# The first gather table: scaling in place on ScalarE and subtracting on GpSimd, in sixteen pieces

## The chip, the cores and the metric

The kernel runs on one core of one Trainium2 chip. The core has a matrix engine (TensorE, "PE" in the profile), three engines for elementwise work (VectorE "DVE", ScalarE "ACT", GpSimd "POOL"), and SyncE ("SP"), which here issues DMAs. Every engine works through its own list of instructions in order; semaphores hold an instruction back until what it needs has been done by another engine. The metric is the device time in microseconds of one execution; lower is better.

## The reference, cut to what matters

The reference propagates node features seven times over a random graph of N = 10000 nodes and E = 160000 edges (D = 128 features), and then runs one self-attention block over the eight "hop" vectors of each node.

```
K = 7
h = x; toks = [x]
for _ in range(K):
    msg = h[src] * deg_inv_sqrt[src, None] * deg_inv_sqrt[dst, None]
    h = segment_sum(msg, dst, N)
    toks.append(h)
...                       # layer norm, attention over the 8 tokens, readout
```

## The kernel before, in words

**Tables.** A hop gathers rows of a table of 79 blocks of 128 nodes. Each table row holds a node's 128 scaled features as two float16 halves, "high" (columns 0 to 127) and "low" (columns 128 to 255): high is the scaled feature rounded to float16, low is what the rounding left. The scale is a power of two, so it can be applied exactly. `tab0` is the table of the first hop. Its float32 source `y` is `x` times `deg_inv_sqrt`; it lies in the storage of `tab1` (the profile therefore calls it `tab` too), which the first hop overwrites later.

**Stages.** Four stages follow each other: pass A (about 45 to 364 us of the span) sorts the 160000 edges by block of their destination, in 25 chunks of 50 columns; `decode` and the first `place` unpack them; seven hops (from about 411 us) gather and scatter on TensorE; attention comes last.

**Pass A, one chunk.** The tile library's scheduler merges the instruction streams of neighbouring chunks; what it gave each engine is a fixed list. In terms of tiles, chunk after chunk:

- VectorE makes a one-hot `oh` (line 204, 128x3950), TensorE counts it into `U` (line 301, 50 matmuls of 79 columns), ScalarE copies that to `U2` (line 314).
- VectorE multiplies `ux = oh * U2` (line 217); TensorE sums it into `R` (lines 222 and 223); VectorE reduces `R` to ranks `rk` (line 226) and compares them into `ro0`, `ro9`, `ro17` (line 337, three instructions).
- The right-hand sides `o0`, `o9`, `o17` are filled by VectorE (line 210) and, for `o9` and `o17`, half by ScalarE with 32 small instructions (line 327).
- TensorE multiplies `ro` by `o` into `ta` (line 341, 50 matmuls, 18 with `o0`, 16 with `o9`, 16 with `o17`), and VectorE adds `ta` up into `TT` (line 305).

`o0`, `o9` and `o17` have one buffer each, so the next chunk's may be written only once TensorE has used them. `oh` has two buffers, so the `oh` of a chunk may be written only once ScalarE has read the one two chunks back.

**The first table** is made inside pass A: at `ch == 2` the program calls `first_table`. A maximum over all of `y` (line 190) gives the scale `q`; then four times, for 20, 20, 20 and 19 blocks, `to_table` (lines 160 to 163) makes the halves and `rows` (lines 165 to 170) has SyncE write them to DRAM (`tabd`, and `tabh` for the last blocks). The first to read them there are the gathers on GpSimd's queue (line 591) in hop 1. The scheduler put ScalarE's part of the table in the middle of its line 327 work for chunk 2, after 13 of the 32 instructions.

Of the kernel before, what the change touches and what calls it, by code (L numbers as in the profile page):

```python
# [14 lines left out]
AF = mybir.ActivationFunctionType  # L15
ALU = mybir.AluOpType
# [27 lines left out]
class Hops:  # L44
# [114 lines left out]

    def to_table(self, y, tab, q, t0, t1):  # L160

        self.nc.scalar.activation(tab[:, t0:t1, 0:128], y, AF.Copy, scale=q)
        self.nc.vector.scalar_tensor_tensor(tab[:, t0:t1, 128:256], y, q, tab[:, t0:t1, 0:128], op0=ALU.mult, op1=ALU.subtract)

    def rows(self, i, tab, t0, t1, eng):
        eng.dma_start(self.tabd[i][t0 * 128:t1 * 128, :].rearrange("(t p) w -> p t w", p=128), tab[:, t0:t1, :])
# [1261 lines left out]
```

## Time and profile before

| | |
|---|---|
| time, median of 3 runs | 4046.84 us (4045.33 to 4047.72) |
| the profiled execution's own time | 4047.25 us |
| its span, from the first to the last instruction | 4045.5 us |
| busy share PE / PEld / DVE / ACT / POOL | 91% / 75% / 75% / 69% / 46% |
| mean granted TensorE clock | 0.975 |

How to read it: a timeline row gives start and duration in us, engine, line, operation, `out<-in`, the shapes, and in brackets the engine's idle time just before and what ended it. Several instructions may be merged into one row (`x4`); its time then runs from the first start to the last end. Neighbouring instructions of an engine overlap a little in the records (by about 0.1 us), so the distance between two starts, not the duration, is what an instruction adds to its engine's list. A row of a window table gives, for a stretch of the span, its length, the busy time of each engine, the granted TensorE clock (1.00 is full speed), the DMA share and GB/s. The chain of waits is the sequence of work that ended last, followed back from the end.

### The profile page before, as it was taken

To read this page: it belongs to the slowest core of one execution; us is meant where nothing else is said; L and a number is where in the kernel's file an instruction comes from. 1 tells how busy PE (TensorE), PEld (TensorE's weight loads), DVE (VectorE), ACT (ScalarE), POOL (GpSimd) and SP (SyncE) were. 2 spreads that over 40 slices of the span, in tenths; PEclk is the share of its full clock that TensorE was granted. 3 is DMA by queue.
4 is the path that set the end of the run, shared out by engine and by line. 5 is a ranking of instruction groups with operands and counts; after the bars stand their busy time and mean duration, and the time that the engine had idled before them with its cause. 6 is when DMAs were issued, how large, how long until landed. Compare 5 with 4: busy or idle time off the path is not lost.

```text
span 4045.5 us, 166006 instructions
## 1 busy us (share of the span) xinstructions
PE 3685.5 (91%) x69042; PEld 3017.9 (75%) x69042; DVE 3041.9 (75%) x6973; ACT 2785.1 (69%) x6934; POOL 1853.3 (46%) x2493
## 2 busy tenths in 40 slices
PE   4776899999889999999999999999999999999996
PEld 3665677777667777777777777777777887888885
DVE  8999988888766666666666666666664555999998
ACT  6674577777656666666666666666666778888884
POOL 0000344444465556555665565665556662222222
PEclk8988999999999999999999999999999999999997
DMA  3100454555466666666666666666667661222220
GB/s 97 37 2 1 158 171 164 175 169 170 142 180 184 186 187 184 185 187 179 188 186 185 184 186 186 185 186 185 185 182 223 187 185 52 73 78 79 73 74 23
DMA packets 320887, 590.64 MB, mean 146 GB/s; under 512 B 56779, under 2 KB 214697, under 8 KB 314873
## 3 DMA queue, kind: packets, MB, share of 16 engines
q1 hardware_dynamic: 281225, 501.46, 40.0%
q0 software_dynamic: 35616, 73.01, 8.0%
q8 instruction: 542, 8.88, 0.9%
q10 hardware_dynamic: 3280, 5.45, 0.5%
q14 instruction: 224, 1.84, 0.1%
HBM read 451.66 MB, written 128.06 MB: 143 GB/s over the span
## 4 chain that ended last, share of the span: by engine, by line
PE 65%; DVE 22%; issue 4%; another core or an unknown queue 3%; DMA 3%; ACT 2%; POOL 1%; SPq 0%; DVEq 0%; POOLq 0%; ACTq 0%
PE acc L645 21%; PE p L667 20%; DVE eb L670 5%; PE acc L631 3%; PE pv L1088 3%; PE po L1099 3%; PE pu L1077 3%; PE ta L341 2%; PE tm L420 2%; DVE s L617 2%; PE pt L1067 1%; DVE ro L337 1%; DVE oh L204 1%; DVE R L210 1%
## 5 line engine op out<-in xcount | busy, mean ns | idle before, releaser
L670 ACT CAST eb<-p 128x512 f16<-128x512 f32 x3494 | 1822.3, 599 | 824.7 <-PE p L667 522.1
L667 PE MATMUL p<-tab,w 128*32 128x256 f16 x39312 | 1306.9, 275 | 108.1 <-DVE eb L670 64.2
L667 PEld LDWEIGHTS <-w 128*32 128x32 fp8e3 x39312 | 997.1, 96 | 336.8 <-issue 280.8
L645 PE MATMUL acc<-eb,w 128*128 128x256 f16 (+1 forms) x9828 | 1198.0, 273 | 0.1
L645 PEld LDWEIGHTS <-w 128*128 128x128 fp8e4 x9828 | 949.1, 98 | 153.4 <-issue 38.8
L670 DVE CAST eb<-p 128x512 f16<-128x512 f32 x1420 | 928.5, 686 | 76.3 <-PE p L667 64.0
L617 DVE TENSOR_REDUCE s<-acc 128x128 f32<-128x256 f32 x553 | 234.2, 424 | 706.3 <-PE acc L645 342.5
L591 POOL DMA_INDIRECT og<-tabh,oidx x546 | 601.5, 1102 | 351.3 <-POOL og L601 175.7
L591 POOL DMA_INDIRECT og<-tabd,oidx x546 | 562.6, 1030 | 303.5 <-issue 123.7
L703 POOL TENSOR_SCALAR r<-s,ctok 128x128 f32<-128x128 f32 x553 | 399.3, 722 | 574.1 <-DVE s L617 523.4
L327 ACT ACTIVATE o<-oh,d2s 128x79 f16<-128x79 f16 x800 | 204.7, 372 | 80.8 <-PE ta L341 80.8
L1113 ACT ACTIVATE junk<-tab 128x128 f32<-128x128 f32 x625 | 245.1, 394 | 0.0
L1099 PEld LDWEIGHTS po<-v,pT 128*128 128x128 f32 x1250 | 161.0, 195 | 42.7 <-issue 27.4
L1171 POOL TENSOR_TENSOR p<-e,in 128x512 f32<-128x512 f32 (+1 forms) x40 | 40.8, 1021 | 331.5 <-DVE e L1169 300.5
L341 PE MATMUL ta<-o,ro 128*128 128x158 f16 x1250 | 119.8, 268 | 77.8 <-DVE ro L337 77.8
L697 DVE SCALAR_TENSOR_TENSOR tab<-s,c,tab 128x128 f16<-128x128 f32 x474 | 170.3, 359 | 14.6
L1088 PE MATMUL pv<-Wv,xT 128*128 128x131 f32 x1250 | 175.5, 283 | 4.7 <-ACT xT L1068 4.1
L341 PEld LDWEIGHTS <-ro 128*128 128x128 f16 x1250 | 114.7, 114 | 82.1 <-DVE ro L337 82.0
L1099 PE MATMUL po<-v,pT 128*128 128x128 f32 x1250 | 168.7, 279 | 5.5 <-DVE o L1105 5.5
L1088 PEld LDWEIGHTS pv<-Wv,xT 128*128 128x128 f32 x1250 | 152.8, 191 | 21.4 <-issue 8.2
L125 POOL MEMSET eb<- 128x520 f16 x10 | 8.2, 852 | 341.1 <-PE ta L341 341.1
L631 PE MATMUL acc<-og,w 128*128 128x256 f16 x546 | 153.9, 282 | 0.0
(314 smaller groups left out, 4650.8 us busy)
## 6 DMA issues: line engine op xcount, KB each, us to landing
w<-gsd SPq DMA_DIRECT2D x468, 592.0 KB
gsd<-w SPq DMA_DIRECT2D x78, 592.0 KB
rb<-srow SPq DMA_DIRECT2D x78, 576.0 KB
tok<-r SPq DMA_DIRECT2D x546, 64.0 KB
tab<-tok SPq DMA_DIRECT2D x273, 128.0 KB
tabd<-tab SPq DMA_DIRECT2D x469, 64.0 KB
og<-tabh,oidx POOLq DMA_INDIRECT x546
og<-tabd,oidx POOLq DMA_INDIRECT x546
```

What stands on the lines that cost most here:

```text
L327: A.activation(o[:, j - a, NK:, i], oh[:, j, :, i], AF.Copy, scale=d2s[:, c0:c0 + 1])
L341: T.matmul(ta, ro[:, j - a, :, i], o[:, j - a, :, i], start=j + i == 0, stop=j + i == NP)
L591: self.nc.gpsimd.indirect_dma_start(out=o, out_offset=None, in_=src[0] if i == NI else src[1], in_offset=bass.IndirectOffsetOnAxis(ap=self ...
L617: self.nc.vector.tensor_reduce(s, acc[:, 0:256].rearrange("p (h d) -> p d h", h=2), axis=X, op=ALU.add)
L631: T.matmul(acc[0][:, :256], W, og()[i], start=start, stop=stop)
L645: T.matmul(acc[0][:, :m], w[:, J * 128:(J + 1) * 128], e[:, j, :m], start=first and J == 0, stop=J == NG - 1 and not (first or late))
L667: T.matmul(p[32 * q:32 * q + 32, j], w[:, NJ * 128 + s * CAP:NJ * 128 + (s + 1) * CAP].bitcast(F8G), tab[:, s, :], start=True, stop=True)
L670: (A.copy if evac(jj) else V.tensor_copy)(e[:, :n, 0:256], p[:, :n].rearrange("p j h d -> p j (h d)"))
L703: self.nc.gpsimd.tensor_scalar(r, s, ct[:, t:t + 1], None, op0=ALU.mult)
L1088: T.matmul(p[:, g - a, :], S[i]["xT"][:, g, :], Wv, start=True, stop=True)
L1099: T.matmul(p[:, g - a, :], PT[i % 2][:, g, :], S[i]["v"][:, g, :128], start=True, stop=True)
L1113: A.activation(j, S[i]["x"][:, g, :], AF.Square, bias=S[i]["x"][:, g, 0:1], scale=-1.0, accum_out=S[i]["sq"][:, g:g + 1])
```

## The change

`to_table` now goes through its blocks five at a time (16 pieces: 15 of five blocks, 640 elements in each partition, and one of four, 512). In each piece ScalarE multiplies `y` by `q` in place in float32 (after's line 165), ScalarE copies the product to the high half, rounding it to float16 (line 166), and GpSimd subtracts the high half from the product into the low half (line 167). Before, ScalarE made the high half straight from `y`, and VectorE computed `y * q - high`, in four instructions each. The DMAs, `first_table` and everything else are the same; line numbers behind `to_table` are four higher in the changed kernel.

```diff
     def to_table(self, y, tab, q, t0, t1):
 
-        self.nc.scalar.activation(tab[:, t0:t1, 0:128], y, AF.Copy, scale=q)
-        self.nc.vector.scalar_tensor_tensor(tab[:, t0:t1, 128:256], y, q, tab[:, t0:t1, 0:128], op0=ALU.mult, op1=ALU.subtract)
+        for i in range(0, t1 - t0, 5):
+            a, b = t0 + i, min(t1, t0 + i + 5)
+            z = y[:, i:i + b - a]
+            self.nc.scalar.activation(z, z, AF.Copy, scale=q)
+            self.nc.scalar.copy(tab[:, a:b, 0:128], z)
+            self.nc.gpsimd.tensor_tensor(tab[:, a:b, 128:256], z, tab[:, a:b, 0:128], op=ALU.subtract)
```

The scheduler's lists for TensorE and SyncE are the same as before. Those of the other three differ only around the table. VectorE's list before, from the last instructions ahead of the table on; the number at a name's end tells buffers apart (`oh_872`, `o9_1161`, `o17_1162`, `ta_1200` belong to chunk 2, `oh_1085`, `o0_1334`, `ux_1313`, `rk_1332` to chunk 3, `oh_1259` to chunk 4), and the brackets name the engines whose semaphores an instruction waits for:

```order
L210 TENSOR_TENSOR o9_1161<-oh_872,d1_270 128x8x158
L163 SCALAR_TENSOR_TENSOR tab0_239<-tab1_64,q2_1061,tab0_239 128x20x128 [waits Activation_49] x3
L163 SCALAR_TENSOR_TENSOR tab0_239<-tab1_64,q2_1061,tab0_239 128x19x128 [waits Activation_49]
L210 TENSOR_TENSOR o17_1162<-oh_872,d1_270 128x8x158
L305 TENSOR_REDUCE TT_264<-ta_987 128x79
L337 TENSOR_TENSOR ro17_1239<-rk_1158,io2_217 128x2048
L204 TENSOR_TENSOR oh_1259<-key_269,io2_217 128x3950 [waits DVE_49,Activation_49]
L217 TENSOR_TENSOR ux_1313<-oh_1085,U2_1257 128x3950 [waits Activation_49]
L210 TENSOR_TENSOR o0_1334<-oh_1085,d1_270 128x9x158 [waits PE_49]
L210 TENSOR_TENSOR o9_1335<-oh_1085,d1_270 128x8x158 [waits PE_49]
L226 TENSOR_REDUCE rk_1332<-R_1312 128x50 [waits PE_49]
L337 TENSOR_TENSOR ro0_1375<-rk_1332,io2_217 128x2304 [waits DVE_49]
```

The same place in the changed kernel (chunk 2 is now `oh_872`, `o9_1201`, `o17_1202`, `ta_1240`; chunk 3 `oh_1125`, `o0_1374`, `ux_1353`, `rk_1372`; chunk 4 `oh_1299`):

```order
L214 TENSOR_TENSOR o9_1201<-oh_872,d1_270 128x8x158
L214 TENSOR_TENSOR o17_1202<-oh_872,d1_270 128x8x158
L309 TENSOR_REDUCE TT_264<-ta_987 128x79
L341 TENSOR_TENSOR ro17_1279<-rk_1198,io2_217 128x2048
L214 TENSOR_TENSOR o0_1374<-oh_1125,d1_270 128x9x158 [waits DVE_49,PE_49]
L793 TENSOR_SCALAR sinv_247<-sinv_247 128x1 [waits DVE_49]
L214 TENSOR_TENSOR o9_1375<-oh_1125,d1_270 128x8x158 [waits DVE_49,PE_49]
L208 TENSOR_TENSOR oh_1299<-key_269,io2_217 128x3950 [waits DVE_49,Activation_49]
L221 TENSOR_TENSOR ux_1353<-oh_1125,U2_1297 128x3950 [waits Activation_49]
L214 TENSOR_TENSOR o17_1376<-oh_1125,d1_270 128x8x158 [waits PE_49]
L230 TENSOR_REDUCE rk_1372<-R_1352 128x50 [waits PE_49]
L341 TENSOR_TENSOR ro0_1415<-rk_1372,io2_217 128x2304 [waits DVE_49]
```

The four table instructions are gone; `o0_1374` and `o9_1375` of chunk 3 now stand ahead of `oh_1299`. Up to `ro0` of chunk 3 the two lists hold the same instructions but for the four; behind it they are the same.

ScalarE's list at the table before:

```order
L327 ACTIVATE o9_1161<-oh_872,d2s_272 128x79 x12
L162 ACTIVATE tab0_239<-tab1_64,q2_1061 128x20x128 [waits DVE_49]
L162 ACTIVATE tab0_239<-tab1_64,q2_1061 128x20x128 x2
L162 ACTIVATE tab0_239<-tab1_64,q2_1061 128x19x128
L327 ACTIVATE o9_1161<-oh_872,d2s_272 128x79 x3
L327 ACTIVATE o17_1162<-oh_872,d2s_272 128x79 [waits PE_49]
L327 ACTIVATE o17_1162<-oh_872,d2s_272 128x79 x15
L314 ACTIVATE U2_1257<-U_1087 128x158 [waits PE_49]
```

and in the changed kernel (the pair of two scalings and two copies comes eight times in all; its first and last stand here):

```order
L331 ACTIVATE o9_1201<-oh_872,d2s_272 128x79 x12
L165 ACTIVATE tab1_64<-tab1_64,q2_1061 128x640 [waits DVE_49]
L165 ACTIVATE tab1_64<-tab1_64,q2_1061 128x640
L166 CAST tab0_239<-tab1_64 128x5x128 [waits Activation_49] x2
L165 ACTIVATE tab1_64<-tab1_64,q2_1061 128x640
L165 ACTIVATE tab1_64<-tab1_64,q2_1061 128x512
L166 CAST tab0_239<-tab1_64 128x5x128 [waits Activation_49]
L166 CAST tab0_239<-tab1_64 128x4x128 [waits Activation_49]
L331 ACTIVATE o9_1201<-oh_872,d2s_272 128x79 x3
L331 ACTIVATE o17_1202<-oh_872,d2s_272 128x79 [waits PE_49]
L331 ACTIVATE o17_1202<-oh_872,d2s_272 128x79 x15
L318 ACTIVATE U2_1297<-U_1127 128x158 [waits PE_49]
```

Thirty-two instructions stand where four stood, ahead of the same 19 of line 327 (now 331) and the same `U2`; each copy waits for its scaling, and another scaling or copy stands between the two. On GpSimd the 16 subtractions stand ahead of five memsets of `eb`, which wait for the end of pass A, and of the first gathers of hop 1.

## The prediction

> **What bounds the kernel now.** The page first: which engine is full where.
>
> ```profile
> PE   4776899999889999999999999999999999999996
> DVE  8999988888766666666666666666664555999998
> PE 65%; DVE 22%; issue 4%; another core or an unknown queue 3%; DMA 3%; ACT 2%; POOL 1%; SPq 0%; DVEq 0%; POOLq 0%; ACTq 0%
> ```
>
> A slice is 101 us. TensorE is full from the fifth slice on, VectorE in the first ones: pass A, where the table is made, is VectorE's stage. Next the chain of waits over pass A, in order of time (start, us, what).
>
> ```profile
> 90.25 11.05 DVE tab L163 x4
> 102.18 3.62 DVE ro L337 x3
> 105.79 2.12 DVE oh L204
> 107.92 2.13 DVE ux L217
> 110.05 3.07 DVE o L210 x4
> 113.73 3.60 DVE ro L337 x3
> ```
>
> The four instructions that the change takes from VectorE lie on the chain with 11.05 us. Whether VectorE could make up a delay later is read from the window table (VectorE's busy time is the third pair of numbers) and from the waits:
>
> ```profile
> 200.00:250.00 50.00, 38.37 (x513) 36.02 (x512) 49.15 (x47) 35.20 (x141) 0.00 (x0) 0.86 0.01 2
> DVE rk L226 <- PE R L223: 6.4, 14, 1.0
> ```
>
> VectorE works 49.15 of 50 us there, so nothing later repays a delay, and none can be hidden: what moves the `ro0` of chunk 3 (113.7 us), behind which both lists are the same, moves the end of pass A and with it the kernel's end. The question is thus when that `ro0` starts in the changed kernel. ScalarE works 35.20 of 50, so it has room over a chunk, but it has to deliver inside it.
>
> **The change part by part.** (1) Off VectorE: the stretch from the table's start to the next instruction.
>
> ```profile
> 87.00 9.26 ACT L162 ACTIVATE tab<-tab,q 128x2560 f16<-128x2560 f32 x4
> 90.17 11.13 DVE L163 SCALAR_TENSOR_TENSOR tab<-tab,q,tab 128x2560 f16<-128x2560 f32 x4
> 96.17 4.89 ACT L327 ACTIVATE o<-oh,d2s 128x79 f16<-128x79 f16 x19
> 101.22 0.81 DVE L210 TENSOR_TENSOR o<-oh,d 128x1264 f16<-128x1264 f16 x1
> ```
>
> 101.22 - 90.17 = 11.05 us. With nothing else, this would be the gain.
>
> (2) Onto ScalarE: 16 scalings and 16 copies for 4 instructions. Their price comes from starts of its neighbours, a per-partition scale (line 183) and a constant one (lines 287 and 288):
>
> ```profile
> 24.78 1.25 ACT L287 ACTIVATE d<-it 128x1250 f16<-128x1250 int32 x1 [0.17 <-DVE it L286]
> 25.93 1.23 ACT L288 ACTIVATE d2s<-it 128x1250 f32<-128x1250 int32 x1
> 27.07 22.01 ACT L183 ACTIVATE tab<-tab,disT 128x128 f32<-128x128 f32 x75
> 48.99 1.28 ACT L243 CAST wl<-W 128x500 f16<-128x500 f32 x3
> ```
>
> Line 183: (48.99 - 27.07)/75 = 0.292 us for 128 elements. Line 162: 96.17 - 87.00 = 9.17 us for four with 10112 elements in all. Both together give 0.833 ns an element and 0.186 us for each instruction. A constant scale: 25.93 - 24.78 = 1.15 us for 1250 elements, of which 0.108 is fixed; a copy is taken at that. So a scaling of 640 costs 0.719, a copy 0.641, the last pair (512) 0.612 + 0.535; 15 x 1.360 + 1.147 = 21.55 us. The table leaves ScalarE at 87.00 + 21.55 = 108.55, 12.4 us later than the 96.17 of before. A copy waits for its scaling, but another instruction runs between them, so I count no gap (a rival below does).
>
> (3) What is queued behind that on ScalarE: 3 instructions of `o9`, 16 of `o17`, then `U2`. The 19 take 4.89 us: 108.55 + 4.89 = 113.44. Who waits: TensorE's `ta` of chunk 2, matmul by matmul; VectorE's `o9_1375` for TensorE's use of `o9` (about 109.6); and VectorE's `oh_1299`, which overwrites what line 327 reads last. VectorE meanwhile goes through `o17`, `TT`, the three `ro` and two `o0` (until about 96.5 us) and then stands still: some 13 us to `o9_1375` and 3 more to `oh_1299`. The 11 us freed are spent on waiting.
>
> (4) From there to `ro0` of chunk 3:
>
> ```profile
> 113.27 0.41 DVE L226 TENSOR_REDUCE rk<-R 128x50 f16<-128x250 f32 x1
> 113.71 3.63 DVE L337 TENSOR_TENSOR ro<-rk,io 128x2304 f16<-128x2304 f16 x3
> 117.25 2.21 DVE L204 TENSOR_TENSOR oh<-key,io 128x3950 f16<-128x3950 f16 x1
> 119.38 2.21 DVE L217 TENSOR_TENSOR ux<-oh,U 128x3950 f16<-128x3950 f16 x1
> 119.52 2.10 PE L301 MATMUL U<-oh,tri 128*128 128x79 f16 x50 [0.58 <-DVE oh L204]
> 121.64 2.03 PE L222 MATMUL R<-ux,id 128*128 128x250 f16 x16
> 123.51 0.19 PE L223 MATMUL R<-wl,id 128*128 128x50 f16 x1
> ```
>
> `oh_1299` starts at about 113.5; `ux` 2.13 later (119.38 - 117.25), 115.63; `R` is done 4.32 after the start of `ux` (123.70 - 119.38), so `rk` starts at 119.98; `ro0` starts 0.44 after `rk` (113.71 - 113.27), at 120.42. `o17_1376` and `TT` (1.1 us) hide under `R`. Before it was 113.71: a delay of 6.7 us. In the lists of front nothing else stands between.
>
> (5) TensorE's clock. This sum takes `U` and `R` at full clock. TensorE will have been nearly idle since about 95 us, with single matmuls 0.25 us apart from 108.9 on. After such a pause before:
>
> ```profile
> 103.58 5.20 PE L341 MATMUL ta<-o,ro 128*128 128x158 f16 x50 [14.48 <-DVE ro L337]
> 103.50:105.00 1.50, 1.42 (x11) 1.43 (x12) 1.50 (x3) 0.00 (x0) 0.00 (x0) 0.50 0.98 289
> 106.00:107.00 1.00, 1.00 (x11) 1.00 (x10) 1.00 (x1) 0.00 (x0) 0.00 (x0) 0.65 0.97 265
> 50.32 6.18 PE L301 MATMUL U<-oh,tri 128*128 128x79 f16 x100 [5.52 <-ACT wl L243]
> ```
>
> The granted clock was 0.50 for about 3.1 us of dense work. 100 matmuls of `U`, mostly at 0.50, took 6.18 us, so 50 take 3.1 instead of 2.10: 1.0 us on the path, and with latencies 1.2. Bounds of the delay: 6.7 (clock already up) to 7.9. The nearest row is the cold one, since the matmuls ahead of `U` are sparse; I take 7.6.
>
> (6) GpSimd: 16 subtractions with two inputs.
>
> ```profile
> L1171 POOL TENSOR_TENSOR p<-e,in 128x512 f32<-128x512 f32 x39 | 40.6, 1041 | 325.2 <-DVE e L1169 294.2 <-ACT junk L1113 31.0
> L1171 POOL TENSOR_TENSOR p<-e,in 128x32 f32<-128x32 f32 x1 | 0.2, 240 | 6.4 <-DVE e L1169 6.4
> 363.99 5.57 POOL L125 MEMSET eb<- 128x520 f16 x5 [341.10 <-PE ta L341]
> 411.04 1.18 POOL L591 DMA_INDIRECT og<-tabh,oidx  x1 [41.49 <-DVE byte L562]
> 408.56 0.33 SPq L430 DMA_DIRECT2D srow<-tbs  x1
> ```
>
> (1041 - 240)/480 = 1.67 ns an element, 1.25 us for 640: less than the 1.36 us in which ScalarE delivers a piece, so the last would end at about 110, 19.8 us of work on an engine that was idle for 341 us. The five table writes on SyncE then wait for GpSimd and start some 10 us later; behind them in SyncE's queue the next DMA is issued at 408.56, and the first gather from the table starts at 411.04: both have some 290 us of room. I count nothing for either.
>
> (7) GpSimd and VectorE at the same time:
>
> ```profile
> 435.44 0.63 POOL L703 TENSOR_SCALAR r<-s,ctok 128x128 f32<-128x128 f32 x1
> 454.96 2.13 DVE L204 TENSOR_TENSOR oh<-kB,io 128x3800 f16<-128x3800 f16 x1
> 455.14 2.61 POOL L703 TENSOR_SCALAR r<-s,ctok 128x128 f32<-128x128 f32 x1 [2.30 <-DVE s L617]
> ```
>
> A GpSimd instruction of 0.63 us took 2.61 when a two-input VectorE one ran; it ended 0.66 after it. VectorE's own kept its 2.13. Here VectorE runs two-input instructions from 90 to 96.5; if GpSimd gets nothing in that time, its 19.8 us end at about 116. That costs nothing if VectorE gives way to nobody, as this row has it. The Trainium skill's page "SBUF — State Buffer", section "SBUF: two separate sides", says that the shared port pair goes to whichever instruction starts first, for its whole length, and that two-input VectorE instructions and reading GpSimd ones block each other fully. The row agrees for one direction; no run here shows the other, a blocked VectorE. By the page the sum would grow by up to two pieces of 1.25 us, from 7.6 to 10.1 us, which is the first rival.
>
> Sum: -11.05 (table off VectorE) + 16 (waiting for ScalarE) + 1.8 (rank chain without cover) + 0.9 (clock) = +7.6 us. The profiled execution took 4047.25 (1.75 of it outside its span), 0.41 above the median: 4054.85 against it, 4054.4 against the median.
>
> **The rivals.** A: GpSimd's pieces still run when `oh_1299` and `ux_1353` start, and hold VectorE up by as much as a piece each. For it: the blocked stretch from 90 to 96.5 makes GpSimd late enough (116 against 113.5). Against it: the 2.13 us of the row above. Price up to 2 x 1.25, so a delay of 8.5 to 10.4, about 4056.3. It decides from the point where GpSimd ends after 113.5.
>
> B: the copies' waits cost ScalarE its overlap. A dependent pair of small instructions in attention shows what a wait on the own engine costs:
>
> ```profile
> 3454.56 0.23 ACT L1219 ACTIVATE ry<-rv 128x32 f32<-128x32 f32 x1
> 3454.82 0.23 ACT L1220 ACTIVATE ry<-ry 128x32 f32<-128x32 f32 x1
> ```
>
> The second starts 0.03 after the first has ended, instead of 0.09 ahead. 32 times 0.12 is 3.8 us: a delay of 10.5 to 11.7, 4057.9. Against it: these stand directly behind each other, the pieces do not.
>
> C, the other sign: ScalarE is done in time, VectorE never waits, and the 11.05 us are gained: 4035.8. It turns at the point where the sum above is zero, a table done by 101.9, that is 14.9 us for 32 instructions or 0.47 us each; 640 elements at 0.833 ns alone are 0.53. No row shows ScalarE that fast.
>
> D: the shift changes the rhythm of the later chunks. VectorE waited 14 times for `R`, 6.4 us in all, when TensorE's clock was low. Were most of that to vanish, the delay would be about 2.5: 4049.3; it may as well grow.
>
> **How the numbers follow.** The forecast (ScalarE late, 6.7 to 7.9 us and small change) has 0.57, A 0.20, B 0.12, D 0.07, C 0.04. 0.2% of this time, about what a measurement of this kernel can tell from no change, is 8.1 us, which lies just above the forecast's middle: of its 0.57 I put 0.22 above. Slower by over 0.2%: 0.22 + 0.19 (A) + 0.12 (B) = 0.53. Within: 0.35 + 0.01 + 0.07 = 0.43. Faster: 0.04. The range from 4051.5 (clock up, a little of D) to 4058.5 (the upper end of B) leaves out C, most of D and little else. The likeliest case alone: 4053.5 to 4054.8.
>
> **What would show it.** In the changed profile: scalings and copies at 0.72 and 0.64 us from start to start, ScalarE's line 331 resuming at 108.5; VectorE idle for some 13 us ahead of `o9` and 3 ahead of `oh`; `ro0` at 120.4 to 121.7; then the same chunk length as before, and every later stage shifted by the same amount. GpSimd ending before 113.5 would rule A out. Wrong would be: resuming near 112 (B), VectorE waiting for POOL (A), or a pass A that ends at a shift other than `ro0` of chunk 3 has (D).

## The result

| | before | changed |
|---|---|---|
| median of 16 runs | 4046.15 us (4038.85 to 4051.12) | 4053.55 us (4047.36 to 4061.5) |
| ratio | | 1.0019, 95% interval 1.0012 to 1.0026 |
| profiled execution: span | 4045.5 us | 4052.8 us |
| first `eb` memset, which waits for the end of pass A | 363.99 | 372.58 |
| first gather of hop 1 | 411.04 | 419.64 |

The changed kernel is 7.4 us slower, clear of no change, and just inside the 0.2% (8.1 us) that the prediction took for what can be told from no change. All of it arises in pass A: its end moved by 8.6 us, the first gather by as much, and the span by 7.3.

The chain of waits over pass A of the changed kernel, in order of time (eight of its pieces):

```profile
85.97 1.41 ACT tab L165 x2
...
104.77 1.34 ACT tab L165 x2
107.24 2.10 ACT o L331 x9
109.42 2.65 ACT o L331 x10
112.08 2.23 DVE oh L208
114.36 3.49 PE U L305 x50
117.85 2.34 PE R L226 x16
120.70 1.37 DVE ro L341
```

Where four VectorE instructions stood in the chain, ScalarE's table stands now, then its 19 instructions of `o9` and `o17`, then `oh`, `U`, `R` and `ro0` of chunk 3. The timeline of the same stretch, ScalarE first, then TensorE's `ta` of chunk 2, GpSimd and VectorE:

```profile
85.85 1.53 ACT L165 ACTIVATE tab<-tab,q 128x640 f32<-128x640 f32 x2
107.14 4.91 ACT L331 ACTIVATE o<-oh,d2s 128x79 f16<-128x79 f16 x19
107.58 4.81 PE L345 MATMUL ta<-o,ro 128*128 128x158 f16 x19 [11.07 <-ACT o L331]
88.08 32.50 POOL L167 TENSOR_TENSOR tab<-tab,tab 128x640 f16<-128x640 f32 x16 [65.13 <-ACT tab L166]
89.87 7.01 DVE L341 TENSOR_TENSOR ro<-rk,io 128x2304 f16<-128x2304 f16 x3
96.81 4.10 DVE L214 TENSOR_TENSOR o<-oh,d 128x1422 f16<-128x1422 f16 x2
108.41 1.20 DVE L214 TENSOR_TENSOR o<-oh,d 128x1264 f16<-128x1264 f16 x1 [7.44 <-PE ta L345]
112.08 2.22 DVE L208 TENSOR_TENSOR oh<-key,io 128x3950 f16<-128x3950 f16 x1 [2.47 <-ACT o L331]
114.23 3.40 DVE L221 TENSOR_TENSOR ux<-oh,U 128x3950 f16<-128x3950 f16 x1
117.56 2.01 DVE L214 TENSOR_TENSOR o<-oh,d 128x1264 f16<-128x1264 f16 x1
120.25 0.42 DVE L230 TENSOR_REDUCE rk<-R 128x50 f16<-128x250 f32 x1 [0.46 <-PE R L227]
120.70 3.63 DVE L341 TENSOR_TENSOR ro<-rk,io 128x2304 f16<-128x2304 f16 x3
```

Two things are to be seen. VectorE waits 7.44 us for TensorE (whose `ta` had waited 11.07 us for ScalarE's `o9`) and 2.47 for ScalarE, and `ro0` starts at 120.70 instead of 113.71. And its own instructions have become longer: the three `ro` take 7.01 us instead of 3.62, `ux` 3.40 instead of 2.21, while GpSimd's 16 pieces take 32.5 us instead of the 20 estimated. That the two engines hold each other up, in both directions, e4 and e5 below show by themselves.

The table itself began 1.15 us earlier than in the profile before (85.85 against 87.00), though nothing ahead of it had changed; over all ten profiles but that of e4 this start lies between 85.76 and 87.47 us. The comparisons below therefore use the distance from the start of ScalarE's table to `ro0` of chunk 3: 113.71 - 87.00 = 26.7 us before, 120.70 - 85.85 = 34.9 us after, a difference of 8.1.

### The profile page after: what moved, and what is told of

It is laid out like the page before. It is cut to its first block, busy times and chain, and to the rows that moved or that the text cites. A ratio compares the mean times of both kernels' runs of the same rounds, so it can differ in the third digit from the quotient of the medians.

```text
span 4052.8 us, 166053 instructions
## 1 busy us (share of the span) xinstructions
PE 3685.0 (91%) x69042; PEld 3017.5 (74%) x69042; DVE 3038.2 (75%) x6969; ACT 2796.5 (69%) x6962; POOL 1880.7 (46%) x2509
## 4 chain that ended last, share of the span: by engine, by line
PE 64%; DVE 22%; issue 5%; another core or an unknown queue 3%; ACT 3%; DMA 2%; POOL 1%; SPq 0%; DVEq 0%; POOLq 0%; ACTq 0%
PE acc L649 20%; PE p L671 18%; DVE eb L674 6%; PE pv L1092 3%; PE acc L635 3%; PE po L1103 3%; PE pu L1081 3%; PE ta L345 2%; DVE s L621 2%; PE pt L1071 2%; PE tm L424 2%; DVE mx L702 1%; DVE oh L208 1%; DVE tab L700 1%
## 5 line engine op out<-in xcount | busy, mean ns | idle before, releaser
L1092 PEld LDWEIGHTS pv<-Wv,xT 128*128 128x128 f32 x1250 | 153.2, 191 | 21.3 <-issue 8.2
L1191 POOL COPY pT<-t 32x512 f32<-32x512 f32 (+1 forms) x160 | 95.5, 597 | 122.8 <-DVE rx L1207 84.3
```

Source lines behind the costliest of these rows:

```text
L1092: T.matmul(p[:, g - a, :], S[i]["xT"][:, g, :], Wv, start=True, stop=True)
```

## The experiments

Eight kernels ran, in two groups of four, each group on one chip beside runs of the kernel before. On the first group's chip the kernel before took 3887.72 us, on the second's 4047.64; each ratio is against the before of its own chip. Microseconds over before are what the ratio is above 1, times that median (so 7.7 for the changed kernel, whose medians differ by 7.4). The intervals reach some 3 to 5 us to either side, so times alone do not separate runs that are closer than that; the last two columns, from one profile each, do it better.

| run | ratio (95%) | us over before | table start to `ro0` of chunk 3 | over before there |
|---|---|---|---|---|
| before (profile) | 1 | 0 | 26.7 | 0 |
| changed (profile) | 1.0019 (1.0012 to 1.0026) | 7.7 | 34.9 | 8.1 |
| e1: subtractions on VectorE | 1.0019 (1.0010 to 1.0028) | 7.4 | 35.0 | 8.2 |
| e2: scaling and subtraction on GpSimd | 1.0034 (1.0022 to 1.0045) | 13.2 | 24.5 | -2.3 |
| e3: four pieces | 1.0030 (1.0019 to 1.0040) | 11.7 | 38.0 | 11.3 |
| e5: before, with idle GpSimd work added | 1.0038 (1.0024 to 1.0052) | 14.8 | 41.1 | 14.4 |
| e6: changed, once more | 1.0024 (1.0014 to 1.0033) | 9.7 | 35.5 | 8.8 |
| e4: no subtractions | 1.0028 (1.0018 to 1.0037) | 11.3 | 34.8 | 8.1 |
| e7: four pieces, VectorE subtracts | 1.0015 (1.0006 to 1.0024) | 6.1 | 31.6 | 4.9 |
| e8: before, two table pieces later | 0.9988 (0.9979 to 0.9997) | -4.9 | 22.7 | -4.0 |

**e1: is it ScalarE, whoever subtracts?**

```diff
-            self.nc.gpsimd.tensor_tensor(tab[:, a:b, 128:256], z, tab[:, a:b, 0:128], op=ALU.subtract)
+            self.nc.vector.tensor_tensor(tab[:, a:b, 128:256], z, tab[:, a:b, 0:128], op=ALU.subtract)
```

> The changed kernel with the 16 subtractions on VectorE instead of GpSimd; ScalarE's part is untouched. Theory (ScalarE's late table sets the time): VectorE does its 11 to 12 us of subtractions inside the 13 us in which it waits, ScalarE resumes line 331 some 21.4 us after it began the table, ro0 of chunk 3 comes as late as in the changed kernel, and the time is 6 to 8 us over the kernel before. Rival 1 (the gain off VectorE was made and GpSimd's port took it back): without GpSimd, but with the 11 us back on VectorE, 11 us or more over the kernel before if the two add, or back at 0 if the port was the only cost. Rival 2 (GpSimd holding VectorE up adds to the wait for ScalarE): 2 to 4 us less than the changed kernel, that is 3 to 5 us over before.

VectorE's timeline there:

```profile
109.34 0.82 DVE L214 TENSOR_TENSOR o<-oh,d 128x1264 f16<-128x1264 f16 x1 [0.23 <-PE ta L345]
113.00 2.22 DVE L208 TENSOR_TENSOR oh<-key,io 128x3950 f16<-128x3950 f16 x1 [2.85 <-ACT o L331]
115.14 2.21 DVE L221 TENSOR_TENSOR ux<-oh,U 128x3950 f16<-128x3950 f16 x1
121.26 0.42 DVE L230 TENSOR_REDUCE rk<-R 128x50 f16<-128x250 f32 x1 [2.95 <-PE R L227]
121.71 3.63 DVE L341 TENSOR_TENSOR ro<-rk,io 128x2304 f16<-128x2304 f16 x3
```

With all of its 11 us back, VectorE is as late as in the changed kernel: the work went into the wait, which shrank to 0.23 us ahead of `o9`. By the distance from the table's start (86.76) to `ro0`, 35.0 us, both rivals of the expectation fall; the time, 7.4 us (3.9 to 10.9), leaves out 0 and, narrowly, 11, but would not by itself leave out 4. `ux` takes its 2.21 again, and `rk` still comes no earlier, because TensorE sets it: from `oh` to `rk` it is 8.26 us here and 8.17 in the changed kernel. `R` starts 3.30 us after `U` here and 3.33 there (114.36 and 117.69), so what GpSimd adds to `ux` in that profile is hidden behind `U` at TensorE's low clock.

**e4: no subtraction at all.** The low halves stay zero: the subtraction line is left out, and one memset clears them at the start.

> The changed kernel without any subtraction: the low halves of the first table stay zero (cleared once at the start), which leaves out that part of the computation, so neither VectorE nor GpSimd does anything for them. Theory (ScalarE's late table sets the time, GpSimd's hold on VectorE is hidden behind it): still 6 to 8 us over the kernel before, the same as the changed kernel, although 11 us of work are simply gone. Rival (GpSimd's pieces cost something in the changed kernel): 1 to 3 us less than the changed kernel.

The clearing and a VectorE instruction beside it, then the table's start, VectorE's two waits and `ro0`:

```profile
11.11 9.19 POOL L181 MEMSET tab<- 128x10112 f16 x1
11.75 8.62 DVE L75 TENSOR_SCALAR ci<-ci 128x128 int32<-128x128 int32 x1
91.56 1.53 ACT L165 ACTIVATE tab<-tab,q 128x640 f32<-128x640 f32 x2
114.12 0.82 DVE L214 TENSOR_TENSOR o<-oh,d 128x1264 f16<-128x1264 f16 x1 [12.82 <-PE ta L345]
117.79 2.22 DVE L208 TENSOR_TENSOR oh<-key,io 128x3950 f16<-128x3950 f16 x1 [2.85 <-ACT o L331]
126.35 3.63 DVE L341 TENSOR_TENSOR ro<-rk,io 128x2304 f16<-128x2304 f16 x3
```

The first two rows are what the expectation had left out. Beside the clearing memset, VectorE's instruction of line 75, 0.41 us long in the kernel before, ends only with the memset; the work behind it comes late, and the whole table began 4.6 us later than in the profile before (91.56). The 11.3 us over before hold that too. Counted from the table's start, `ro0` is 34.8 us off, 8.1 over before: with the subtraction gone from every engine the delay is the same. And VectorE's two waits are now 12.82 and 2.85 us, the 13 and 3 of the prediction's step 3. The changed kernel has 34.9 in its first profile and 35.5 in the one run beside e4 (e6), so GpSimd's hold cost it between nothing and some 0.7 us.

> The changed kernel itself once more, beside the others. 6 to 8 us over the kernel before, ro0 of chunk 3 some 33 to 35 us behind the start of ScalarE's table (26.7 in the kernel before).

e6 came out above both of its ranges, at 9.7 us (5.7 to 13.4) and 35.5. In its profile GpSimd held not only `ux` but also `oh`, which took 3.20 us instead of 2.22:

```profile
112.64 3.20 DVE L208 TENSOR_TENSOR oh<-key,io 128x3950 f16<-128x3950 f16 x1 [2.84 <-ACT o L331]
115.76 3.40 DVE L221 TENSOR_TENSOR ux<-oh,U 128x3950 f16<-128x3950 f16 x1
```

From `oh` to `rk` it was 8.78 us there, some 0.5 more than in e1.

**e3 and e7: fewer, longer pieces.** Both take 20 blocks a piece; e3 subtracts on GpSimd, e7 on VectorE.

```diff
-        for i in range(0, t1 - t0, 5):
-            a, b = t0 + i, min(t1, t0 + i + 5)
+        for i in range(0, t1 - t0, 20):
+            a, b = t0 + i, min(t1, t0 + i + 20)
```

> The changed kernel with four pieces of 20 and 19 blocks instead of 16. ScalarE has 24 instructions less: 18.0 us for the table instead of 21.4. Theory (a microsecond of ScalarE's table is a microsecond of the time): 3.4 us less than the changed kernel, 3 to 5 us over the kernel before. But GpSimd's pieces now take some 5.5 us each and start later, so if they hold VectorE up in both directions the oh and ux of chunks 4 and 3 meet one of them: 1 to 5 us of the 3.4 are lost again, 5 to 9 us over before.

> Four pieces, with the subtractions on VectorE: ScalarE's table as in the four-piece run (18.0 us), GpSimd's hold taken away. Theory (a microsecond of ScalarE's table is a microsecond of the time): 3.4 us less than with sixteen pieces, 3 to 5 us over the kernel before. If it stays at 9 to 12 us over, like the four pieces with GpSimd, the long pieces on GpSimd were not what cost there.

ScalarE's part first, the same in both, from e7, with e7's `ro0`; then VectorE in e3:

```profile
86.72 4.73 ACT L165 ACTIVATE tab<-tab,q 128x2560 f32<-128x2560 f32 x2
104.68 4.90 ACT L331 ACTIVATE o<-oh,d2s 128x79 f16<-128x79 f16 x19
118.29 3.63 DVE L341 TENSOR_TENSOR ro<-rk,io 128x2304 f16<-128x2304 f16 x3
```

```profile
96.18 10.94 DVE L214 TENSOR_TENSOR o<-oh,d 128x1422 f16<-128x1422 f16 x2 [0.37 <-PE ta L345]
107.11 5.60 DVE L214 TENSOR_TENSOR o<-oh,d 128x1264 f16<-128x1264 f16 x1
112.63 6.79 DVE L208 TENSOR_TENSOR oh<-key,io 128x3950 f16<-128x3950 f16 x1
```

ScalarE's table takes 17.96 us instead of 21.3, and in e7 `ro0` comes 3.4 us earlier than in e1 (31.6 against 35.0): a microsecond for a microsecond, as the theory has it. In time e7 is 6.1 us over before (2.4 to 9.7), above the 3 to 5 expected but 3.6 below e6 on the same chip; the times are too coarse to say more. In e3 the same 3.4 us are gained on ScalarE, and 6.4 are lost to GpSimd: its pieces of over 5 us each hold up `o9` (5.60 us instead of 0.81) and `oh` (6.79 instead of 2.21). The loss, and the 11.7 us over before, are larger than the expectation allowed (1 to 5, and 5 to 9), since two pieces in a row, not one, meet VectorE on the path.

**e5: the price of GpSimd by itself.** Into the kernel before, 20 subtractions whose results nobody reads:

```diff
+        for i in range(0, t1 - t0 - 1, 4):
+            n = 2 if t1 - t0 - i >= 4 else 1
+            z, h = y[:, i:i + 2 * n], tab[:, t0 + i:t0 + i + 2 * n, 0:128]
+            o = self.ebuf[0][:, 0:n, 0:256].rearrange("p a (b d) -> p a b d", b=2)
+            self.nc.gpsimd.tensor_tensor(o, z.rearrange("p (a b) d -> p a b d", b=2), h.rearrange("p (a b) d -> p a b d", b=2), op=ALU.subtract)
```

> The kernel before, with 20 GpSimd subtractions of 512 elements added in pass A that nobody uses (same operands as in the change, result into a buffer that is overwritten later); VectorE's, ScalarE's and TensorE's lists are those of before. VectorE is full there, so this prices GpSimd's hold on it by itself. If VectorE gives way to nobody (the one row quoted in the prediction): 0 us over before, GpSimd's pieces stretched. If the two shut each other out in both directions, each piece costs VectorE about its own 1.1 us: 12 to 22 us over before.

VectorE's timeline there, over the table and two chunks, and the 20 pieces on GpSimd:

```profile
90.33 14.72 DVE L163 SCALAR_TENSOR_TENSOR tab<-tab,q,tab 128x2560 f16<-128x2560 f32 x4
106.89 6.26 DVE L342 TENSOR_TENSOR ro<-rk,io 128x2304 f16<-128x2304 f16 x3
119.25 6.99 DVE L215 TENSOR_TENSOR o<-oh,d 128x1422 f16<-128x1422 f16 x4
126.16 0.31 DVE L310 TENSOR_REDUCE TT<-ta 128x79 f32<-128x158 f32 x1
126.83 5.83 DVE L342 TENSOR_TENSOR ro<-rk,io 128x2304 f16<-128x2304 f16 x3
88.26 48.02 POOL L168 TENSOR_TENSOR eb<-tab,tab 128x512 f16<-128x512 f32 x20 [65.31 <-ACT tab L162]
```

VectorE's list is that of before, and up to `ro0` of chunk 3 each instruction with two inputs in SBUF is longer by 0.9 to 1.0 us (`o`: 6.99 us for the four that took 3.15), while the reduction from PSUM keeps its 0.31. Of the 20 pieces 16 had begun when `ro0` of chunk 3 started at 126.83, and the last ended at 136.28: 14.4 us for 16 pieces is 0.9 us a piece. "VectorE gives way to nobody" is refuted.

**e2: ScalarE in time, GpSimd busy for longer.** ScalarE makes the high half in one step; GpSimd scales in place and subtracts.

```diff
-            self.nc.scalar.activation(z, z, AF.Copy, scale=q)
-            self.nc.scalar.copy(tab[:, a:b, 0:128], z)
+            self.nc.scalar.activation(tab[:, a:b, 0:128], z, AF.Copy, scale=q)
+            self.nc.gpsimd.tensor_scalar(z, z, q, None, op0=ALU.mult)
```

> ScalarE makes the high half in one step of 16 pieces, as many elements as before the change, and GpSimd does both the scaling in place and the subtraction. The lateness of ScalarE is taken away: its table takes 16 x 0.72 = 11.5 us instead of 21.4, so oh of chunk 4 is released some 10 us earlier. If ScalarE alone set the time and GpSimd cost VectorE nothing: ro0 of chunk 3 some 3 us earlier than in the kernel before, and the time about 3 us below it (4043). If a piece of GpSimd's holds up each two-input VectorE instruction that it meets by a piece (1.2 to 1.4 us), and VectorE is now on the path while GpSimd works some 35 us: 5 to 15 us more than that, 2 to 12 us over the kernel before.

Four rows of its timeline, of ScalarE, VectorE (two) and GpSimd:

```profile
87.42 11.50 ACT L165 ACTIVATE tab<-tab,q 128x640 f16<-128x640 f32 x16
103.75 2.22 DVE L208 TENSOR_TENSOR oh<-key,io 128x3950 f16<-128x3950 f16 x1 [0.90 <-ACT o L331]
133.44 3.42 DVE L221 TENSOR_TENSOR ux<-oh,U 128x3950 f16<-128x3950 f16 x1
175.11 1.26 POOL L167 TENSOR_TENSOR tab<-tab,tab 128x512 f16<-128x512 f32 x1
```

ScalarE is out of the way at 98.8 us, and `ro0` of chunk 3 is 2.3 us earlier than before, near the 3 expected. But GpSimd works until 176 us, beside a VectorE that is now on the path, and takes some 17 us in the following chunks: the end of pass A, at 379.54, is 15.1 us over before, counted from the table's start. The end result, 13.2 us over before, is a little above the 2 to 12 expected.

**e8: a version that beats both.** If VectorE bounds pass A, its table work should go where it waits for TensorE. ScalarE's part stays as before; VectorE's pieces for blocks 0 to 19 and 20 to 39 stand behind the last `ro` of pass A and behind the first `ux` of `place`, held there by a scale that is computed as `0 * (element of that ro or ux) + q`. `low_half` issues the VectorE instruction that is taken out here, over the blocks it is given; `LATE` is 40; the call in `place` is left out.

```diff
-        self.nc.vector.scalar_tensor_tensor(tab[:, t0:t1, 128:256], ...)
+        if t0 >= LATE:
+            self.low_half(y, tab, q, t0, t1)
...
+    def late_piece(self, a, b, after):
+        q = self.ql[:, a // 20:a // 20 + 1]
+        self.nc.vector.scalar_tensor_tensor(q, after, 0.0, self.qk, op0=ALU.mult, op1=ALU.add)
+        self.low_half(self.tab[1].bitcast(F32)[:, a:b, :], self.tab[0], q, a, b)
+        self.rows(0, self.tab[0], a, b, self.nc.sync)
...
+            self.late_piece(0, 20, ro[:, 0, 0, 0:1])
             take(NCH - 1, ta)
...
```

> A version meant to beat both: the kernel before, with ScalarE's part untouched and VectorE's table instructions for blocks 0 to 19 and 20 to 39 moved to two places where VectorE waits for TensorE: behind the last ro of pass A (a wait of 3.15 us) and behind the ux of the first place (3.46 us). Theory (VectorE is the bound of pass A, so what leaves it for a wait is gained): 2 x 2.8 = 5.6 us, less some 0.3 us for two small instructions that hold them there, so 5 us below the kernel before; the two DMAs then start at about 364 and 402 us, ahead of the gathers from tabd at 427. Rival (the waits lengthen by what is put into them, because ScalarE or TensorE was bound there as well): no change, within 1 us.

The two pieces in its timeline, each with the VectorE instruction behind it, and the first gather:

```profile
357.68 2.88 DVE L170 SCALAR_TENSOR_TENSOR tab<-tab,ql,tab 128x2560 f16<-128x2560 f32 x1
360.61 0.32 DVE L321 TENSOR_REDUCE TT<-ta 128x79 f32<-128x158 f32 x1
396.05 2.88 DVE L170 SCALAR_TENSOR_TENSOR tab<-tab,ql,tab 128x2560 f16<-128x2560 f32 x1
399.28 0.42 DVE L242 TENSOR_REDUCE rk<-ur 128x50 f16<-128x250 f32 x1 [0.35 <-PE ur L239]
407.94 1.17 POOL L608 DMA_INDIRECT og<-tabh,oidx  x1 [41.73 <-DVE byte L579]
```

Both pieces lie in waits that were there: the last `TT` of pass A follows at once, and `rk` in `place` still comes 5.6 us after its `ux`, as before. The time fell by 4.9 us (1.2 to 8.5), and 5 were expected. The profile shows a little less of it: the first gather came 3.1 us earlier than before (407.94 against 411.04), 3.6 when counted from the table's start.

## Why the prediction was right

The forecast was 4054.4 us, 7.6 over the median then known; measured were 4053.55 and 7.4. Its likeliest case was that VectorE's freed time is spent on waiting for ScalarE, and e1, e4 and e7 show that. The larger part of its chances (0.53) lay on a slowdown of over 0.2%, though, and the measured one stays just below that. Step by step:

- **What bounds the kernel.** Right: `ro0` of chunk 3 came 7.0 us later, the end of pass A 8.6, the first gather 8.6. The 1.6 between are the rhythm of rival D, on the slow side: VectorE waited 16 times for `R` instead of 14, 7.7 us instead of 6.4. Most of it falls into one chunk, from `ro0` at 237.61 to `ro0` at 250.66: 13.05 us instead of 11.4 to 11.9, with 1.55 us of waiting for `R`.
- **ScalarE's price** (2). Sized 21.55 us, measured 107.14 - 85.85 = 21.29. The copies' waits cost nothing, so rival B is out: it would have brought line 331 near 112.
- **What is queued behind it** (3). The 19 instructions took 4.91, and `oh` began 26.2 us after the table, 26.5 forecast. VectorE's wait was 7.4 + 2.5 us instead of 13 + 3: this term was mis-sized, because step 7 had VectorE untouched by GpSimd, and 5.8 us of what I called waiting were longer `ro` and `o0` instructions; without GpSimd, in e4, the waits are 12.82 + 2.85. On the sum it changes nothing, since `o9_1375` and `oh_1299` wait for ScalarE either way.
- **Rank chain and clock** (4, 5). From `oh` to `rk` 6.5 us at full clock, 0.9 taken for the low one; measured 8.17, that is 1.7 more. (The 1.8 of the sum is not worked out from rows; it is what is left of the 6.7.) `U` took 3.49 instead of 2.10, and `R` 2.50 instead of 2.03: the clock came up later than I thought, some 4.2 us into the dense work (114.36 to about 118.6) instead of 3.1. Three windows of the changed kernel's trace, over `o9` to `oh`, `U` and `R`; the columns are the window's bounds and length, the busy time of PE, PEld, DVE, ACT and POOL with the number of instructions, the granted clock, the DMA share and GB/s:

```profile
109.00:112.00 3.00, 3.00 (x13) 1.25 (x12) 0.62 (x1) 3.00 (x14) 3.00 (x2) 0.50 0.51 149
116.00:117.80 1.80, 1.80 (x29) 1.77 (x27) 1.80 (x2) 1.80 (x9) 1.80 (x1) 0.50 0.25 71
117.80:120.00 2.20, 2.20 (x17) 1.67 (x16) 2.00 (x2) 2.20 (x10) 2.20 (x2) 0.78 0.00 0
```

- **GpSimd** (6). Mis-sized: the shortest piece took 1.39 us, not 1.25, the median 2.0, and the last ended at 120.6, not 110 or 116. The table's DMAs went out up to 123.5 us, and nobody waited for them: that part was right.
- **VectorE and GpSimd** (7). Wrong: the one row quoted showed VectorE's side unharmed because its instruction had started first. Rival A's mechanism was there, with the point that it named (GpSimd past 113.5) passed. It did not set the time in the first profile only because `U`, at the low clock until 117.85, covered the late `ux` (117.63); that was by a hair, and luck. In e6 it cost some 0.5 to 0.7 us. The rule of the Trainium skill, page "SBUF — State Buffer", section "SBUF: two separate sides", that whichever starts first shuts the other out, agrees with e5: 0.9 us of VectorE's time for each piece.
- **Rival C** is out: nothing was gained, since ScalarE did not come near the 14.9 us that it would have needed.

The two errors that mattered, a clock 0.8 us dearer than taken and a rhythm 1.6 us worse, were met by a table that began 1.15 us earlier and a later part of the kernel that gave back 1.3 us; so the profile's agreement is partly luck. Counted from the table's start, `ro0` came 8.1 us later in this profile and 8.8 in e6, both above the bounds of 6.7 and 7.9. The times, 7.4 us and in e6 9.7, lie on either side of the forecast.

## What to carry to other kernels

Work that is taken off a full engine helps only if the engine that takes it delivers in time: price the new owner's list up to the next thing that the full engine waits for, not its share of idle time. Two-input elementwise work on GpSimd is not free beside a busy VectorE: in e5 it cost VectorE 0.9 us for each piece of 512 elements, and on the path longer pieces made it worse (e3 lost 6.4 us by them). Look first for a wait that the full engine already has, and move its own work there: that gave 4.9 us here where the hand-over lost 7.4.

## What the runs showed of the hardware that had not been expected

- A memset of 9.19 us on GpSimd held up a one-input VectorE instruction of 0.41 us until its end (8.62 us, e4).
- VectorE and GpSimd take turns: with both lists full, the three `ro` took 7.01 us instead of 3.62, and the 16 pieces of the changed kernel 32.5 us, where 16 of the shortest (1.39) would be 22. Reductions from PSUM (0.31 and 0.42 us) were not lengthened.
- Single matmuls 0.25 us apart, from 107.6 to 112.4 us, did not raise TensorE's clock: it stayed at 0.50 and was still there some 4.2 us into the dense work that followed (0.50 in the window from 118.20 to 118.60, 1.00 from 118.90 to 119.30).
- The same kernel took 3887.72 us on one chip and 4047.64 on another. Pass A is alike on both (it ended at 373.80 in e1, on the first, and at 372.58 in e6, on the second); a part of the hops moved 201 GB/s on the one (e1's profile, 1200 to 2700 us) and 185 in the profile of before, an execution of 4047.25 us. The window of e1, and then that of before, in the columns of the windows above:

```profile
1200.00:2700.00 1500.00, 1488.14 (x31193) 1260.51 (x31186) 1118.64 (x2443) 1028.13 (x2031) 959.12 (x1406) 1.00 0.67 201
```

Before:

```profile
1200.00:2700.00 1500.00, 1422.07 (x28612) 1158.46 (x28601) 991.84 (x2247) 971.01 (x1864) 899.71 (x1291) 1.00 0.64 185
```

What makes the chips differ was not tried.
